# Block transposes through DRAM for the second batch of an attention and token-mixing kernel

## The chip, the cores and the metric

One Trainium2 chip, one core of it. The metric is the device time of one execution in microseconds (us); the median of several runs is given, and one more execution is profiled. TensorE (PE) multiplies matrices and also transposes by multiplying with an identity; VectorE (DVE), ScalarE (ACT) and GpSimd (POOL) work elementwise; SyncE (SP) issues almost all transfers, in one queue and in order. The five work side by side and wait for each other by semaphores.

## The reference

Four batches, 8 heads, 768 positions, head dimension 64. First attention in a window of 16 positions to both sides, with 24 more columns, one for each block of 32 positions (the maximum of its keys, the mean of its values). Then a mixer: an MLP over the tokens (768 to 256 to 768) with a residual, and an MLP over the channels (512 to 1536 to 512) with a residual.

```python
k_sum = k.reshape(B, H, nb, block, D).max(axis=3)
v_sum = v.reshape(B, H, nb, block, D).mean(axis=3)
scores_l = scale * np.matmul(q, k.transpose(0, 1, 3, 2))
mask_l = np.abs(pos[:, None] - pos[None, :]) < window
scores_s = scale * np.einsum('bhsd,bhnd->bhsn', q, k_sum) + np.log(block)
scores_all = np.concatenate([np.where(mask_l, scores_l, -1e9), scores_s], axis=-1)
a = np.exp(scores_all - np.max(scores_all, axis=-1, keepdims=True))
a = a / (np.sum(a, axis=-1, keepdims=True) + 1e-09)
x = np.matmul(a, np.concatenate([v, v_sum], axis=2))   # heads side by side: (B, S, 512)
...
xt = x.transpose(0, 2, 1)
h = np.maximum(xt @ w_tok1, 0.0) @ w_tok2
u = x + h.transpose(0, 2, 1)
h2 = np.maximum(u @ w_ch1, 0.0) @ w_ch2
return (u + h2).astype(np.float32)
```

## The kernel before, in words

The channel MLP is the bulk. It runs batch by batch, each batch in two halves of its tokens (512 and 256 columns; 384 and 384 in the last batch), and each half in 12 slots, one for each 128 of the 1536 hidden channels: `ch1` (12 matmuls into a bank hp), relu and a split into a high and a low part (ACT L851, DVE L856), `ch2` (12 matmuls added to banks acc). Numbers are carried as two float32r parts, so that each product takes three matmuls.

The attention of the next batch runs inside the MLP of the batch before it. A batch has four pairs of heads (p in the code, `NP` = 4 for each batch), and each pair two halves g of its tokens. The steps, 20 for a batch, are

- "s", `scores`: 24 matmuls (L428) into two banks sc, the minimum with the mask on DVE (L442) into a tile e, the exponential in place on ACT (L452). The tile e is 128 queries by 2 heads by 3 blocks of 128 columns, 120 of them used.
- "e", `turn` or `turn_blocks`: e must stand with its columns on the partitions for the next product; the result is eT.
- "a", `weighted`: 48 matmuls av (L559) of eT and v, scaled on DVE (L571) into x, and for some batches `turn_x` behind it. After it the next pair's v is loaded.

`ORDER` and `LATER` are two lists of these steps: `ORDER` puts the next pair's scores between the two "e" steps of a pair, `LATER` puts both "e" steps ahead of them. When all pairs are done, `tok1x` (PE L736, with splits xs and ws on ACT L717 and POOL L722) and `tok2` (PE L771, L779) make the token MLP and u. The first channel matmul of a batch needs u of all four pairs, of its half. The half with the higher tokens is made in slots 2 to 5 of the batch's own MLP. In the first batch's MLP the attention of the second is spread over a stretch from unit 20 to unit 30 (`a0`, `a1`, units of 256 columns; 36 in a batch), that is slots 10 to 17, since the weights are still being prepared ahead of it; in the later ones it is spread over units 0 to 29. `tok1x` stands in slots 20 and 22, `tok2` in slot 23 of the first batch's MLP.

Tiles come from rings: a tag such as "e" has 3 buffers, and the i-th tile of a tag can be written when tile i - 3 has been read for the last time. e, eT (from the second batch on), xb and the first half's xT all take buffers of "e". The order of instructions on each engine is written down beforehand: every piece of work is given to `Plan` with its engine, an assumed duration and a rank, a list scheduler runs through them with these durations (`RATE` and `LAND` for transfers), and each engine's queue is then fixed in the order of the assumed starts. Ranks go from `R_H` (scores, flips, weighted sums) down to `R_W` (the channel matmuls). `FAR` is the first batch that is turned by `turn_blocks` and `turn_x`.

```python
def att_step(b, s, behind=()):
    kind, hp, g = (LATER if b >= FAR else ORDER)[s]
    p = b * NP + hp
    if kind == "e":
        (turn_blocks if b >= FAR else turn)(p, g)
    elif kind == "a":
        weighted(p)
        if b >= FAR:
            turn_x(b, hp)
...
# in the loop over slots
if b >= FAR and u1s[p] == slot + 1: fetch_x(b, 1, p)
...
if b + 1 >= FAR: fetch_x(b + 1, 0, p)
tok2(b + 1, 0, p)
```

Of the kernel before, what the change touches and what calls it, by code (L numbers as in the profile page):

```python
# [188 lines left out]
def tile_attention_mixer(  # L189
# [22 lines left out]
    def sbuf(shape, tag, name, bufs, dtype=F32):  # L212
        return plan.slot(sb, shape, dtype, tag, name, bufs)
# [188 lines left out]
    def scores(p, g, behind=()):  # L402
# [3 lines left out]
        e = e_t[p, g] = sbuf([P, 2, HS], "e", f"e_{p}_{g}", 3)  # L406
        if p >= FAR * NP:

# [59 lines left out]
                )  # L468


    FAR = 2
    PARTS = [(j, i) for j in range(2) for i in range(TT // 2)]

    def turn(p, g):
# [126 lines left out]
# [10 lines that stand above are left out]
# [17 lines left out]
    def turn_x(b, p):  # L628

        x2, a = x_t[b, p]  # L630
        e = sbuf([P, S], "e", f"xb_{b}_{p}", 3)
        add(
            "dve", 1.05,
            lambda: nc.vector.transpose(
                e.t.rearrange("p (t c) -> p t c", c=P), x2.t[:, :, a, :]
            ),
            reads=x_keys(b, p), writes=[(e, 0)], rank=R_ATT,
        )
        for half, nt in enumerate(HT[b]):
            cs = slice(H0[b][half], H0[b][half] + nt)  # L640
            away = xa_t[b, half, p] = plan.slot(
                dram, [P, nt], F32, f"xaway{nt}", f"xaway_{b}_{half}_{p}", 8
            )
            add(
                "sp", 0.4, lambda away=away, cs=cs: nc.sync.dma_start(out=away.t, in_=e.t[:, cs]),
                reads=[(e, 0)], writes=[(away, 0)], kb=nt // 2,
            )

    def fetch_x(b, half, p):
        tag, bufs = (("e", 3), ("ot", 2))[half]  # L650
        slot = xT_t[b, half, p] = sbuf([P, HT[b][half]], tag, f"xT_{b}_{half}_{p}", bufs)
        fetch(xa_t.pop((b, half, p)), slot, lambda: slot.t, HT[b][half] // 5)
# [489 lines left out]
    for b in range(B):  # L1142
# [12 lines left out]
        for slot, (half, f) in enumerate(seq):  # L1155
            state["phase"] = half
            for p in range(NP):
                if b >= FAR and u1s[p] == slot + 1:
                    fetch_x(b, 1, p)
# [31 lines left out]
            if not last:  # L1191
# [7 lines left out]
                for p in range(NP):  # L1199
                    if slot == t2s[p]:  # L1200
                        if b + 1 >= FAR:
                            fetch_x(b + 1, 0, p)
# [66 lines left out]
```

## Time and profile before

| | |
|---|---|
| median of three runs | 581.9 us (580.58 to 582.2) |
| profiled execution, first to last instruction | 579.3 us; its own time is not listed apart from the runs |
| PE, DVE, ACT, POOL busy | 565.0, 288.2, 216.0, 154.1 us |
| mean granted TensorE clock | 0.994 of full speed |
| packets of under 512 B | 86640 of 116778 |
| bytes moved, mean rate | 75.89 MB, 131 GB/s |

Rows of groups read: line, engine, operation, written and read tile, shape and count; then busy time, mean of one in ns; then the engine's idle time just before them and what ended it. Rows of a timeline read: start and length in us, engine, line, operation, count. Rows of windows read: the stretch, its length, busy us and instructions of PE, of PE's weight loads, of DVE, ACT and POOL, the granted clock, the DMA engines' busy share and the rate in GB/s. SPq is SP's queue of transfers; a row there is the time that issuing took, not that of the transfer. L12 is line 12 of the kernel.

### The profile page before, as it was taken

To read this page: it belongs to the slowest core of one execution; us is meant where nothing else is said; L and a number is where in the kernel's file an instruction comes from. 1 tells how busy PE (TensorE), PEld (TensorE's weight loads), DVE (VectorE), ACT (ScalarE), POOL (GpSimd) and SP (SyncE) were. 2 spreads that over 40 slices of the span, in tenths; PEclk is the share of its full clock that TensorE was granted. 3 is DMA by queue.
4 is the path that set the end of the run, shared out by engine and by line. 5 is a ranking of instruction groups with operands and counts; after the bars stand their busy time and mean duration, and the time that the engine had idled before them with its cause. 6 is when DMAs were issued, how large, how long until landed. Compare 5 with 4: busy or idle time off the path is not lost.

```text
span 579.3 us, 12315 instructions
## 1 busy us (share of the span) xinstructions
PE 565.0 (98%) x4701; PEld 500.2 (86%) x4701; DVE 288.2 (50%) x872; ACT 216.0 (37%) x697; POOL 154.1 (27%) x191
## 2 busy tenths in 40 slices
PE   7889999989999999999999999999999999999997
PEld 4678888768999988878899988888799999999997
DVE  3698799997563255644743336452543222112112
ACT  4777565436474343322333224222434111111110
POOL 0236586743033310000085010100085022005000
PEclk9999999989999999999999999999999999999999
DMA  8954568653565027846775127746454012001001
GB/s 281 325 159 129 182 200 262 220 164 129 188 190 161 18 76 197 230 121 188 204 192 131 23 55 189 195 139 139 117 146 81 1 34 59 1 1 54 1 1 54
DMA packets 116778, 75.89 MB, mean 131 GB/s; under 512 B 86640, under 2 KB 100080, under 8 KB 116720
## 3 DMA queue, kind: packets, MB, share of 16 engines
q1 hardware_dynamic: 116432, 74.72, 45.6%
q8 instruction: 37, 0.61, 0.4%
q10 hardware_dynamic: 288, 0.39, 0.2%
q14 instruction: 21, 0.17, 0.1%
HBM read 57.59 MB, written 15.73 MB: 127 GB/s over the span
## 4 chain that ended last, share of the span: by engine, by line
PE 82%; DVE 11%; DMA 3%; issue 2%; ACT 1%; SPq 0%; POOL 0%; DVEq 0%; ACTq 0%
PE acc L882 31%; PE hp L839 30%; PE t1q L736 5%; PE up L779 4%; PE av L559 4%; PE sc L428 4%; DMA w<-in_w_ch 2%; DVE wb L1067 2%; DVE wp L1060 1%; PE et L490 1%; PE warm L1108 1%; DVE wp L1053 1%; DVE wb L1060 1%; DVE vs L384 1%; DVE e L442 1%
## 5 line engine op out<-in xcount | busy, mean ns | idle before, releaser
L882 PE MATMUL acc<-h,w2h 128*128 128x512 f32 (+2 forms) x768 | 207.1, 340 | 2.2 <-DVE h L856 2.2
L839 PE MATMUL hp<-u,w1h 128*128 128x512 f32 (+2 forms) x768 | 192.7, 338 | 0.0
L882 PEld LDWEIGHTS acc<-h,w2h 128*128 128x128 f32 x768 | 135.8, 189 | 17.0 <-DVE h L856 3.4
L839 PEld LDWEIGHTS hp<-u,w1h 128*128 128x128 f32 x768 | 132.6, 189 | 12.3 <-issue 1.3
L856 DVE SCALAR_TENSOR_TENSOR h<-hp,h 128x512 fp32r<-128x512 f32 (+2 forms) x96 | 53.1, 553 | 153.8 <-ACT h L851 153.8
L839 PE MATMUL hp<-u,w1l 128*128 128x512 f32 (+2 forms) x384 | 129.1, 336 | 0.3 <-POOL w1l L1095 0.3
L882 PE MATMUL acc<-h,w2l 128*128 128x512 f32 (+2 forms) x384 | 129.1, 336 | 0.0
L851 ACT ACTIVATE h<-hp 128x512 fp32r<-128x512 f32 (+2 forms) x96 | 46.9, 488 | 201.4 <-PE hp L839 200.4
L452 ACT ACTIVATE e<-e,den 128x120 f32<-128x120 f32 x192 | 73.3, 385 | 48.6 <-DVE den L442 41.1
L839 PEld LDWEIGHTS hp<-u,w1l 128*128 128x128 f32 x384 | 72.5, 189 | 6.6 <-POOL w1l L1095 0.7
L882 PEld LDWEIGHTS acc<-h,w2l 128*128 128x128 f32 x384 | 72.6, 189 | 5.2
L943 POOL TENSOR_TENSOR ot<-ot,u 128x512 f32<-128x512 f32 (+2 forms) x28 | 27.9, 1021 | 116.8 <-DVE ot L935 116.8
L442 DVE CUSTOM_DVE_ANT_0 e<-sc,mask_sb 128x120 f32<-128x120 f32 x192 | 41.4, 277 | 13.7 <-PE sc L428 10.9
L779 PE MATMUL up<-wt2h,t 128*128 128x256 f32 (+2 forms) x128 | 37.6, 351 | 0.5 <-DVE xT L795 0.5
L411 POOL MEMSET e<- 128x48 f32 x16 | 2.2, 138 | 130.1 <-DMA away<-e 69.5
L452 ACT ACTIVATION_READ_ACCUMULATOR e<-e,den 128x1 f32 x192 | 36.3, 189 | 0.0
L722 POOL TENSOR_TENSOR xs<-x,xs 128x512 fp32r<-128x512 f32 x18 | 23.5, 1304 | 27.8 <-ACT xs L717 27.7
L428 PE MATMUL sc<-k,q 64*64 64x120 f32 x768 | 28.6, 275 | 1.9 <-PE et L490 0.7
L428 PEld LDWEIGHTS sc<-k,q 64*64 64x64 f32 x768 | 21.0, 134 | 10.5 <-issue 6.8
L736 PE MATMUL t1q<-xs,ws 128*128 128x256 f32 x216 | 28.9, 284 | 0.0
L559 PEld LDWEIGHTS av<-v,eT 120*64 120x64 f32 x768 | 24.0, 138 | 4.8 <-issue 2.3
L736 PEld LDWEIGHTS t1q<-xs,ws 128*128 128x128 f32 x216 | 27.3, 191 | 0.3
(73 smaller groups left out, 597.0 us busy)
## 6 DMA issues: line engine op xcount, KB each, us to landing
w<-in_w_ch SPq DMA_DIRECT2D x48, 256.0 KB
k<-in_kw SPq DMA_DIRECT2D x16, 720.0 KB
v<-in_vw SPq DMA_DIRECT2D x32, 288.0 KB
q<-in_q SPq DMA_DIRECT2D x16, 384.0 KB
away<-e SPq DMA_DIRECT2D x16, 384.0 KB
eT<-away SPq DMA_DIRECT2D x64, 96.0 KB
w<-in_w_tok SPq DMA_DIRECT2D x12, 256.0 KB
vb<-in_vb SPq DMA_DIRECT2D x32, 96.0 KB
```

The costliest lines, as they stand in the source:

```text
L428: nc.tensor.matmul(tiles[j].t[c * QT : (c + 1) * QT, i * NC : (i + 1) * NC], lhsT=qt.t[rows, t * QT : (t + 1) * QT], rhs=kt.t[rows, t, :], ...
L442: nc.vector.tensor_tensor_reduce(out=e.t[:, j, i * P : i * P + NC], in0=tiles[j].t[:, i * NC : (i + 1) * NC], in1=mask_sb[:, mv, :], op0=A ...
L452: nc.scalar.activation(ei, ei, AF.Exp, bias=den_t[n].t[:, 1, T : T + 1], scale=-1.0, accum_out=den_t[n].t[:, 0, T : T + 1],)
L559: nc.tensor.matmul(pv[cs, T], lhsT=eT[:NC, T % (TT // 2), cs], rhs=v.t[:NC, 2 * T + c], start=True, stop=True,)
L722: lambda slot=slot, src=src: nc.gpsimd.tensor_tensor(out=slot.t[:, 1], in0=src(), in1=slot.t[:, 0].bitcast(F32), op=ALU.subtract),
L736: nc.tensor.matmul(pt.t[:, 2 * P * k : 2 * P * (k + 1)], lhsT=ws[:, wp, T, ks], rhs=xs[:, xp, T], start=(c == 0 and k == 0 and T == 0 and ...
L779: nc.tensor.matmul(pt.t[:, :nt], lhsT=t1.t[:, part, ks], rhs=w[:, k, h0 : h0 + nt], start=(far and k == 0 and i == 0), stop=(k == DTOK // ...
L839: nc.tensor.matmul(pt.t[:, :nt], lhsT=w[:, c, fs], rhs=us[c].t[:, part], start=(i == 0), stop=(i == len(ops) - 1),)
L851: lambda: nc.scalar.activation(h.t[:, 0], pt.t[:, :nt], AF.Relu),
L856: lambda: nc.vector.scalar_tensor_tensor(out=h.t[:, 1], in0=pt.t[:, :nt], scalar=0.0, in1=h.t[:, 0].bitcast(F32), op0=ALU.max, op1=ALU.sub ...
L882: nc.tensor.matmul(slot.t[:, c0 : c0 + nt], lhsT=w[:, f, o * P : (o + 1) * P], rhs=h.t[:, part], start=(f == 0 and w is w2h and part == 0 ...
L943: lambda view=view, u=u: nc.gpsimd.tensor_tensor(out=view(), in0=view(), in1=u.t[:, 1].bitcast(F32), op=ALU.add),
```

## The change

`FAR` goes from 2 to 1, so the second batch (b = 1) takes the path of the third and fourth.

```diff
-    FAR = 2
+    FAR = 1
```

What this exchanges for b = 1:

- `turn` flips each e on PE (three matmuls with the identity for each head, L490) into a bank and copies it to eT on ACT (L501). `turn_blocks` transposes the 32 by 32 blocks of e in place on DVE (L513), writes the tile to DRAM (away, L517, 384 KB) and fetches it in four transfers (L532, 96 KB each, in runs of 32 numbers), one for each group of 32 partitions, so that the blocks land where the full transpose has them. `scores` also zeroes the unused columns of e on POOL (L411).

```python
def turn_blocks(p, g):
    e = e_t[p, g]
    away = plan.slot(dram, [P, 2 * HS], F32, "away", f"away_{p}_{g}", 3)
    t_sb = sbuf([P, 2, HS], "e", f"eT_{p}_{g}", 3)
    ...
    add("dve", 1.05, lambda: nc.vector.transpose(flat(e.t), flat(e.t)), ...)
    add("sp", 0.4, lambda: nc.sync.dma_start(out=away.t, in_=flat(e.t)), ...)
    fetch(away, t_sb, lambda: flat(t_sb.t), 150)

def fetch(away, slot, view, kb):
    def part(r):
        rows = slice(32 * r, 32 * (r + 1))
        src = away.t.rearrange("(q p) (t k) -> p t q k", p=32, k=P)
        nc.sync.dma_start(
            out=view()[rows].rearrange("p (t q c) -> p t q c", q=P // 32, c=32),
            in_=src[..., rows])
    for r in range(P // 32):
        add("sp", 0.4, lambda r=r: part(r), reads=[(away, 0)], writes=[(slot, r)], kb=kb)
```

- The residual's x was transposed inside `tok2` on PE (L771) into the bank of the token MLP. Now `turn_x` transposes the blocks of x on DVE (L634) into a tile xb and writes both halves to DRAM (xaway, L645), and `fetch_x` brings each back as xT in four transfers. `tok2` adds bank and xT on DVE (L795), copies the high part of u on ACT (L802) and subtracts on DVE or, in the second half, on POOL (L808).
- The steps of b = 1 come in the order `LATER` instead of `ORDER`.

## The prediction

> **What bounds the kernel now.** I read the page first: busy shares, then the chain that ended last.
>
> ```profile
> span 579.3 us, 12315 instructions
> PE 565.0 (98%) x4701; PEld 500.2 (86%) x4701; DVE 288.2 (50%) x872; ACT 216.0 (37%) x697; POOL 154.1 (27%) x191
> PE 82%; DVE 11%; DMA 3%; issue 2%; ACT 1%; SPq 0%; POOL 0%; DVEq 0%; ACTq 0%
> ```
>
> PE is the bound as an average, so an instruction taken off PE is worth its own time, but only where the PE queue has other work ready. The second batch's attention runs inside the first batch's MLP, so the stretch that decides is from its first scores to the first matmul of its MLP. I took that stretch from the timeline of PE, the chain in order of time, and the table by windows.
>
> ```profile
> 128.38 0.85 PE L428 MATMUL sc<-k,q 64*64 64x120 f32 x24
> 145.24 1.55 PE av L559 x48
> 178.88 1.55 PE av L559 x48
> 206.50 0.63 PE L839 MATMUL hp<-u,w1h 128*128 128x512 f32 x2
> 145.00:185.00 40.00, 40.00 (x557) 37.93 (x556) 22.35 (x102) 23.36 (x87) 8.05 (x9) 1.00 0.63 193
> 185.00:205.00 20.00, 20.00 (x148) 18.80 (x147) 6.36 (x14) 6.94 (x15) 8.32 (x8) 1.00 0.07 18
> ```
>
> In the window rows the first pair is length and busy PE. The second batch's scores begin at 128.38, its four pairs of heads finish their weighted sums (L559) from 145.24 to 178.88 + 1.55 = 180.4, one pair every (178.88 - 145.24) / 3 = 11.2 us, and its MLP (512 columns wide) begins at 206.50. PE never idles between 145 and 205. So there are 206.5 - 180.4 = 26.1 us between the last weighted sum and the MLP, all of it filled, and the attention has that much room at most. The third batch starts at 209.35 and has some 125 us of MLP to hide in; the second has only what is left of the first batch's MLP.
>
> **The change, part by part.** Removed from PE: the flips of e (L490), three matmuls for each of 16 tiles, 48 in all, and the residual's transposes (L771), 16 in the first half and 8 in the second.
>
> ```profile
> 135.75 0.82 PE L490 MATMUL et<-identf,e 128*120 128x128 f32 x6
> 136.32 0.36 PE L839 MATMUL hp<-u,w1h 128*128 128x256 f32 x1
> 190.51 0.60 PE L771 MATMUL up<-identf,x 128*128 128x128 f32 x4
> 190.86 0.51 PE L779 MATMUL up<-wt2h,t 128*128 128x512 f32 x1
> ```
>
> Six flips hold the queue 136.32 - 135.75 = 0.57 us, 0.095 each: 48 x 0.095 = 4.6 us. Four residual transposes hold it 0.35 us, 0.088 each: 16 give 1.4, the 8 of the second half 0.7. PE sheds 6.7 us; with the cover intact that is the gain. ACT also loses its 16 copies of eT.
>
> Added elsewhere, from the groups by form and from the tiles' views (shortest/median/longest, ns):
>
> ```profile
> L513 DVE STREAM_TRANSPOSE e<-e 128x768 f32<-128x768 f32 x16 | 15.6, 976 | 11.5 <-ACT e L452 11.2
> L634 DVE STREAM_TRANSPOSE xb<-x 128x768 f32<-128x768 f32 x8 | 7.8, 979 | 0.3
> L411 POOL MEMSET e<- 128x48 f32 x16 | 2.2, 138 | 130.1 <-DMA away<-e 69.5 <-PE av L559 41.5 <-PE et L490 10.3
> L532 SPq DMA_DIRECT2D eT<-away x64: 557/652/3628, 221.0 to 426.3; - x64
> L517 SPq DMA_DIRECT2D away<-e x16: 327/374/593, 214.9 to 420.2; - x16
> L645 SPq DMA_DIRECT2D xaway<-xb x16: 421/497/653, 237.1 to 435.4; - x16
> L532 SPq DMA_DIRECT2D xT<-xaway x64: 557/622/1198, 308.8 to 484.1; - x64
> ```
>
> Per batch: DVE gets 8 x 0.98 + 4 x 0.98 = 11.7 us of block transposes, and in tok2 one more addition for each u. In the second half the subtraction goes to POOL. POOL gets 8 memsets, 1.1 us. All three engines are half idle in these windows (DVE 22.35 of 40 us), so I cost that work at nothing where it stands beside PE, and count it only where it lies in the chain below. SP's queue gets 8 x 0.37 + 32 x 0.65 + 8 x 0.50 + 32 x 0.62 = 47.7 us of issuing, some 27 us of it before the last weighted sum. It is one queue in order: k, q, v, vb and the third batch's preparations wait behind each fetch that waits for its trip to DRAM.
>
> The price is in the latency of one pair of heads. The ring "e" has three buffers, and e, eT and xb now all turn in it. The second e of a pair can be written only when the previous pair's second eT has been read by its weighted sum, so the chain of a pair is closed: weighted sum, scaling, turning x, minimum, exponential, block transpose, write to DRAM, four fetches, weighted sum. Nothing of it runs ahead. The third batch shows it under the same loads of k, q, v and vb:
>
> ```profile
> 209.35 0.85 PE L428 MATMUL sc<-k,q 64*64 64x120 f32 x24
> 230.68 1.55 PE av L559 x48
> 255.42 1.55 PE av L559 x48
> 263.56 0.98 DVE L513 STREAM_TRANSPOSE e<-e 128x768 f32<-128x768 f32 x1
> 264.31 0.69 SPq L270 DMA_DIRECT2D k<-in_kw  x1
> 265.05 0.43 SPq L270 DMA_DIRECT2D q<-in_q  x1
> 265.58 0.38 SPq L517 DMA_DIRECT2D away<-e  x1
> 273.16 1.97 SPq L532 DMA_DIRECT2D eT<-away  x3
> 275.87 0.56 SPq L532 DMA_DIRECT2D eT<-away  x1
> 278.25 1.59 PE av L559 x48
> 305.05 1.55 PE av L559 x48
> ```
>
> From the first scores to the end of the first weighted sum: 230.68 + 1.55 - 209.35 = 22.9 us. From one weighted sum to the next: 278.25 - 255.42 = 22.8 and 305.05 - 278.25 = 26.8. In the first of these the write went out behind k and q, its first fetch came 273.16 - 265.58 = 7.6 us later, the last fetch was issued at 276.43, and the weighted sum at 278.25 is a piece of the chain that ended last: this interval is not just slack in the schedule. Where k and q were farther ahead, the trip was shorter:
>
> ```profile
> 243.74 0.33 SPq L517 DMA_DIRECT2D away<-e  x1
> 247.38 2.67 SPq L532 DMA_DIRECT2D eT<-away  x4
> ```
>
> that is 6.3 us from the write's issue to the last fetch's end. Lower end for a pair: the present 11.2, plus 0.98 and 6.3, less the flips and copies that go (0.57 and some 0.9): 17, and I put 16 so that an overlap is allowed for. Upper end: the mean of 22.8 and 26.8, 24.8. I take 20, nearer to 22.8, since the loads are the same and the ring is the same, and a little below it because PE's order added about 1 us there and the third batch was not pressed for time.
>
> Last weighted sum of the second batch: 128.4 + 22.9 + 3 x 20 = 211.3, instead of 180.4. The first batch's MLP does not wait for it and runs out at 206.5 - 4.6 - 1.4 = 200.5. Behind the last weighted sum lies what the MLP needs: the splits of x for tok1x, tok1x, tok2, and the residual's fetch. The third batch again gives the length:
>
> ```profile
> 327.40 0.69 DVE L808 TENSOR_TENSOR u<-xT,u 128x512 fp32r<-128x512 f32 x1 [0.75 <-ACT u L802]
> 319.02 2.37 SPq L532 DMA_DIRECT2D xT<-xaway  x3
> ```
>
> The last u there is done at 328.1, 328.1 - 306.6 = 21.5 us behind the weighted sum, with MLP matmuls between. Its last fetch of xT ended at 321.4, held back because the fourth xT takes the ring's buffer from the first; addition, copy and subtraction follow (about 2 us, and 2 for landing): 18.9 us at least by that path. Without the MLP in between I take 18.5 and keep 17 and 21.5 as ends. So the second batch's MLP starts at 211.3 + 18.5 = 229.8 instead of 206.5: 23.3 us late, with PE idle for most of 29 us.
>
> After an idle PE the clock is lower for a while:
>
> ```profile
> 117.00:119.00 2.00, 0.18 (x2) 0.16 (x2) 2.00 (x6) 1.12 (x3) 1.19 (x2) 1.00 0.57 198
> 119.00:121.00 2.00, 2.00 (x6) 1.51 (x7) 1.97 (x5) 0.14 (x2) 0.99 (x2) 0.52 0.97 329
> 121.00:123.00 2.00, 2.00 (x7) 1.62 (x6) 2.00 (x4) 0.73 (x2) 1.53 (x2) 0.62 0.58 183
> ```
>
> Granted clock (third column from the right) 0.52 and 0.62 in 4 us cost 2 x 0.48 + 2 x 0.38 = 1.7 us; bounds 0 and twice that, taken once. Sum: +23.3 + 1.7 - 0.7 = +24.3. The third and fourth batches have room (their attention is spread over a whole MLP), so the delay is carried to the end unchanged. The profiled span of 579.3 becomes 603.6. The median of the runs, 581.9, lies 2.6 above the span; I carry that over: 606.
>
> How much of the pair's 20 us is the short runs of the fetches (32 numbers of 4 bytes at a time) shows in the table by windows, whose last two columns are DMA share and GB/s:
>
> ```profile
> 218.00:220.00 2.00, 2.00 (x11) 1.63 (x10) 1.90 (x4) 0.23 (x1) 0.00 (x0) 1.00 0.99 390
> 226.00:228.00 2.00, 2.00 (x14) 1.75 (x13) 0.41 (x2) 0.63 (x2) 0.00 (x0) 1.00 0.79 126
> ```
>
> With k and q under way the queues moved 390 GB/s at a share of 0.99; with fetches of eT alone 126 at 0.79, 160 for full share. 384 KB take 2.5 us at the one rate and 1.0 at the other. At the higher rate the two fetches of a pair would be 3 us shorter, a pair 17 and the time 597. The Trainium skill, "DMA: Bandwidth & Descriptors", section Specifications, gives 512 B as the least transfer for line rate; by that rule the 128 B runs stay at the low rate, the trace agrees (126 against 390), and the sum is the 606 and not the 597. The Trainium skill, "VectorE: DVE Perf Modes", section Rules for kernel authors, also speaks against the change: it sends a 128x128 transpose to TensorE where PSUM will do as its target, which here is the 0.57 us on PE against the trip of 6.3 to 7.6 us.
>
> **The rivals.** *Hidden (faster).* The round trip fits beside the MLP that is left. Then the second batch's MLP starts at 200.5, PE keeps all 6.7 us and the time is 575. It decides by the pair's interval: 200.5 - 18.5 = 182, so (182 - 151.3) / 3 = 10.2 us for a pair; break-even is near 12.5. For it speaks that the planner sets a new order; against it that 11.2 is today's interval without the trip, and that the ring closes the chain. Chance 0.10, of which 0.02 lands within 0.3%.
>
> *Short trip.* The chain of a pair runs at its lower end, 16, and the tail at 17: 128.4 + 22.9 + 48 + 17 = 216.3, 9.8 late, less 0.7: the time is 591. For it speaks the 6.3 us trip; against it the same loads packed into less time. Chance 0.20.
>
> *Queue in order (slower still).* SP waits for one write with the next pair's loads behind it, as where one fetch took 3628 ns to issue. 24.8 for a pair and 21.5 behind: 128.4 + 22.9 + 74.4 + 21.5 = 247.2, 40.7 late, less 0.7 and plus 1.7: 624. Chance 0.12.
>
> **How the numbers follow.** The forecast, 606, has 0.58, with a range of its own of 596 to 616 (a pair at 17 to 23). The range 590 to 620 takes in the short trip and leaves out the hidden case and the upper end of the queue case, 0.18 together. About 0.3%, 1.7 us, is what a measurement of this kernel can tell from no change. Faster 0.08, same 0.02, slower 0.90.
>
> **What would show it.** The profile after: no flips beyond the first batch's 48, 24 block transposes of e and 12 of x, 96 fetches of eT. Weighted sums of the second batch some 20 us apart, the last ending near 211. PE idle, waiting for e, DMA or t1q's splits, some 29 us between 150 and 232, and a dip of the granted clock behind it. The MLP of the second batch starts near 230, everything after keeps its spacing. The prediction is wrong if the weighted sums stand 12 us apart or less, if the first batch's MLP does not run out before they end, or if the second batch's scores start well before 128.

## The result and the profile after

The changed kernel takes 608.8 us (median of 4 runs, 606.8 to 609.25) against 582.05 before: ratio 1.0445, interval 1.0412 to 1.0479. It is slower by 26.8 us. The profiled execution spans 606.5 us, 27.2 more than before.

First the page of the changed kernel: span, busy shares, and from the 40 slices PE's busy tenths and its granted clock.

```profile
span 606.5 us, 12360 instructions
PE 563.1 (93%) x4629; PEld 497.8 (82%) x4629; DVE 302.4 (50%) x888; ACT 209.9 (35%) x681; POOL 158.4 (26%) x203
...
PE   7789999899972579999999999999999999999997
...
PEclk9999999999995778999999999999999999999999
```

PE has 72 instructions fewer and its share falls from 98% to 93%. The two lines of slices (15.2 us each) say where: a hole in slices 13 to 15 (182 to 227 us), with the granted clock down to half in it. Elsewhere the PE line stays within a tenth or two of that of the kernel before. The groups and a tile's view show that the instructions moved as the code says:

```profile
L490 PE MATMUL et<-identf,e 128*120 128x128 f32 x48 | 8.3, 288 | 3.5 <-ACT e L452 3.4
L513 DVE STREAM_TRANSPOSE e<-e 128x768 f32<-128x768 f32 x24 | 23.4, 976 | 14.8 <-ACT e L452 14.4
L532 SPq DMA_DIRECT2D eT<-away x96: 557/654/2144, 138.0 to 454.7; - x96
```

The weighted sums of the second batch and the first matmul of its MLP, from PE's timeline:

```profile
149.32 1.76 PE L559 MATMUL av<-v,eT 120*64 120x64 f32 x48
172.63 1.62 PE L559 MATMUL av<-v,eT 120*64 120x64 f32 x48
195.26 2.19 PE L559 MATMUL av<-v,eT 120*64 120x64 f32 x36 [4.10 <-DMA eT<-away]
...
233.04 0.62 PE L839 MATMUL hp<-u,w1h 128*128 128x512 f32 x2
```

and the end of the attention, from the chain in order of time:

```profile
196.29 5.96 DMA v<-in_vw
...
202.26 1.42 SPq L532
203.73 1.25 SPq L532
...
205.08 3.38 DMA away<-e
208.47 0.56 SPq L532
...
211.17 2.58 DMA eT<-away
213.89 2.20 PE av L559 x36
```

The weighted sums end at 151.1, 174.2, 197.5 and 216.1: 21.7 us apart on the mean (before: 11.2). No PE row stands between the last two in this stretch of the chain: SP's fetches, the write of e to DRAM, the fetch back. The chain puts the last two of the four fetches ahead of that write (1.42 and 1.25 us of issuing against a median of 0.65) behind v's transfer. Before this stretch the chain holds SP's issuing alone, from 180.31 to 193.03. SP's queue there:

```profile
179.10 2.42 SPq L532 DMA_DIRECT2D xT<-xaway  x3
181.57 2.72 SPq L532 DMA_DIRECT2D eT<-away  x4
...
188.34 1.88 SPq L532 DMA_DIRECT2D xT<-xaway  x3
190.26 2.72 SPq L532 DMA_DIRECT2D eT<-away  x4
```

Fetches of x for the second half, which are needed only once the second batch's MLP runs, stand directly ahead of the fetches of eT.

The MLP starts at 233.04 instead of 206.50, 26.5 us later, and that is nearly the whole 27.2. Counted from the second batch's first scores it takes 108.2 us in place of 78.1, which is 30.0 more: in this run the scores began 3.5 us earlier, at 124.88. The windows:

```profile
160.00:180.00 20.00, 18.24 (x219) 17.25 (x217) 12.41 (x44) 8.76 (x33) 4.68 (x6) 1.00 0.87 222
180.00:200.00 20.00, 4.70 (x72) 4.05 (x72) 7.89 (x35) 3.05 (x15) 3.68 (x7) 0.54 0.80 204
200.00:215.00 15.00, 8.66 (x69) 8.24 (x71) 4.88 (x17) 3.52 (x14) 2.82 (x3) 0.73 0.78 171
215.00:233.00 18.00, 15.03 (x81) 12.14 (x79) 6.79 (x11) 5.77 (x11) 7.71 (x7) 0.79 0.59 122
sum 108.00, PE 81.49 PEld 73.09 DVE 56.34 ACT 34.27 POOL 25.96; mean PE 13.58 PEld 12.18 DVE 9.39 ACT 5.71 POOL 4.33
```

The sum is over 125 to 233 (the rows before 160 are left out): PE is idle for 108.0 - 81.5 = 26.5 us there. Of the engines that took the work over, DVE is busy for half of the stretch (56.3 us) and POOL for a quarter. The transfer engines are at 0.78 to 0.87 from 160 to 215, and at 0.59 behind that.

What the ring of three buffers does shows on POOL, whose memset is the first to write a new e (from its timeline):

```profile
174.32 0.14 POOL L411 MEMSET e<- 128x48 f32 x1 [7.42 <-PE av L559]
197.52 0.14 POOL L411 MEMSET e<- 128x48 f32 x1 [9.89 <-PE av L559]
```

So the second e of a pair does wait for the weighted sum of the pair before. It is not the only thing that holds it there: DVE has the scaling of that sum (197.49) and the turning of x (198.09) ahead of the minimum that fills this e (198.99), in its own fixed order.

### The profile page after: what moved, and what is told of

It is laid out like the page before. It is cut to its first block, busy times and chain, and to the rows that moved or that the text cites. A ratio compares the mean times of both kernels' runs of the same rounds, so it can differ in the third digit from the quotient of the medians.

```text
span 606.5 us, 12360 instructions
## 1 busy us (share of the span) xinstructions
PE 563.1 (93%) x4629; PEld 497.8 (82%) x4629; DVE 302.4 (50%) x888; ACT 209.9 (35%) x681; POOL 158.4 (26%) x203
## 4 chain that ended last, share of the span: by engine, by line
PE 67%; DVE 9%; DMA 9%; SPq 6%; ACT 4%; issue 3%; POOL 2%; DVEq 0%; ACTq 0%; POOLq 0%
PE acc L882 26%; PE hp L839 26%; SPq L532 5%; PE av L559 4%; PE up L779 4%; PE t1q L736 3%; PE sc L428 3%; DMA w<-in_w_ch 2%; DMA v<-in_vw 2%; ACT e L452 2%; DVE wb L1067 1%; DVE wp L1060 1%; DVE wp L1053 1%; DMA k<-in_kw 1%; DVE wb L1060 1%
## 5 line engine op out<-in xcount | busy, mean ns | idle before, releaser
L856 DVE SCALAR_TENSOR_TENSOR h<-hp,h 128x512 fp32r<-128x512 f32 (+2 forms) x96 | 53.0, 552 | 151.3 <-ACT h L851 151.2
L779 PE MATMUL up<-wt2h,t 128*128 128x256 f32 (+2 forms) x128 | 39.3, 366 | 3.1 <-ACT t L670 1.6
L559 PE MATMUL av<-v,eT 120*64 120x64 f32 x768 | 29.4, 235 | 11.6 <-DMA eT<-away 10.2
L411 POOL MEMSET e<- 128x48 f32 x24 | 3.3, 138 | 141.0 <-PE av L559 61.8
L559 PEld LDWEIGHTS av<-v,eT 120*64 120x64 f32 x768 | 26.4, 147 | 16.0 <-issue 9.4
L428 PEld LDWEIGHTS sc<-k,q 64*64 64x64 f32 x768 | 21.1, 135 | 21.0 <-issue 17.4
L736 PE MATMUL t1q<-xs,ws 128*128 128x256 f32 x216 | 31.3, 300 | 4.8 <-ACT e L452 2.8
L736 PEld LDWEIGHTS t1q<-xs,ws 128*128 128x128 f32 x216 | 29.4, 206 | 5.8 <-ACT e L452 2.9
```

Of the source, the lines that this page charges most:

```text
L428: nc.tensor.matmul(tiles[j].t[c * QT : (c + 1) * QT, i * NC : (i + 1) * NC], lhsT=qt.t[rows, t * QT : (t + 1) * QT], rhs=kt.t[rows, t, :], ...
L559: nc.tensor.matmul(pv[cs, T], lhsT=eT[:NC, T % (TT // 2), cs], rhs=v.t[:NC, 2 * T + c], start=True, stop=True,)
L736: nc.tensor.matmul(pt.t[:, 2 * P * k : 2 * P * (k + 1)], lhsT=ws[:, wp, T, ks], rhs=xs[:, xp, T], start=(c == 0 and k == 0 and T == 0 and ...
L779: nc.tensor.matmul(pt.t[:, :nt], lhsT=t1.t[:, part, ks], rhs=w[:, k, h0 : h0 + nt], start=(far and k == 0 and i == 0), stop=(k == DTOK // ...
L856: lambda: nc.vector.scalar_tensor_tensor(out=h.t[:, 1], in0=pt.t[:, :nt], scalar=0.0, in1=h.t[:, 0].bitcast(F32), op0=ALU.max, op1=ALU.sub ...
```

## The experiments

Theory A: the chain of one pair of heads through DRAM, closed by the ring of three buffers, sets the pace. Rival B: the order of the steps (`LATER`) does. Rival C: the traffic does, either by the engines' time (C1) or by SP's issuing in order (C2). Intervals below are between the ends of the second batch's weighted sums, as a mean of three.

In all edits `FAR` is split in three: `FAR_E` for e's turning, `FAR_X` for x's, `FAR_O` for the order.

**The order alone.**

```diff
+    FAR_E, FAR_X, FAR_O = 2, 2, 1
```

> Only the order of the second batch's steps is changed to LATER; e is flipped and x transposed on PE as before. Theory A (the closed chain of a pair through DRAM costs the time) expects about the time of the kernel before, 580 to 584 us, weighted sums of the second batch 10 to 13 us apart. Rival B (the order of the steps does it) expects 600 us or more with weighted sums 18 us or more apart. Rival C (SP's queue and the transfers' volume do it) expects 580 to 584 us, as there are no new transfers.

583.0 us, ratio 1.0026 (1.0005 to 1.0048). From PE's timeline, the first and last of the four sums and the MLP's start:

```profile
144.19 1.62 PE L559 MATMUL av<-v,eT 120*64 120x64 f32 x48
...
177.21 1.62 PE L559 MATMUL av<-v,eT 120*64 120x64 f32 x48
207.69 0.63 PE L839 MATMUL hp<-u,w1h 128*128 128x512 f32 x2
```

(177.21 - 144.19) / 3 = 11.0 us apart. The order alone costs a quarter of a per cent, half a per cent at the most. B is out.

**e alone through DRAM.**

```diff
+    FAR_E, FAR_X, FAR_O = 1, 2, 1
```

> e of the second batch goes through DRAM, order LATER; the residual's x stays on PE. Theory A expects most of the loss: weighted sums 19 to 22 us apart, 602 to 608 us. Rival C expects clearly less of the loss, since the write-outs of x (4 x 384 KB) and 32 fetches of x in SP's queue are gone: weighted sums 16 to 18 us apart, 592 to 600 us.

605.0 us, ratio 1.038 (1.0329 to 1.0431). The chain's last rows:

```profile
214.24 2.19 PE av L559 x36
231.63 2.75 PE hp L839 x12
```

The first sum ended at 154.0, so the intervals are 20.8. From the first scores (127.28) to the MLP it takes 104.2 us, 4.0 less than in the changed kernel. Turning e makes most of the loss, 23.6 us on the kernel before as it was measured beside this run. Taking 32 fetches and 8 writes of x out of SP's queue shortened a pair by 0.9 us, where C expected intervals of 16 to 18.

**x alone through DRAM.**

```diff
+    FAR_E, FAR_X, FAR_O = 2, 1, 1
```

> Only the residual's x of the second batch goes through DRAM, order LATER; e is flipped on PE. Theory A expects no stall to speak of, because x's trip is needed only at the end: weighted sums 10 to 14 us apart, 2.1 us of PE work gone, 578 to 583 us. Rival C expects part of the loss, 586 to 592 us, as SP issues 40 more transfers.

590.1 us, ratio 1.015 (1.0117 to 1.0183): A's number failed and C's held. The chain in order of time says by what:

```profile
162.20 8.38 DMA xaway<-xb
...
170.69 0.50 ACT eT L501
...
171.23 1.62 PE av L559 x48
```

ACT's copy of eT waited for the write of x: eT takes the buffer of "e" that xb still held, and this write took 8.4 us to land. Intervals are 14.5 us, just above A's 10 to 14. So a trip that nothing reads for a long time entered the chain through a shared ring.

**eT from another ring.**

```diff
-        t_sb = sbuf([P, 2, HS], "e", f"eT_{p}_{g}", 3)
+        tag, n = ("u0", 4) if p < 2 * NP else ("e", 3)
+        t_sb = sbuf([P, 2, HS], tag, f"eT_{p}_{g}", n)
```

> The whole change, but eT of the second batch takes its four buffers from another ring (u0), so that the second e of a pair need not wait for the weighted sum of the pair before. The first eT must wait for the first batch's first half to be finished (about 145), and part of the splits for tok1x move behind the last weighted sum (some 5 us). Theory A expects weighted sums 13 to 17 us apart, 594 to 604 us. Rival C expects that transfers set the pace: still 19 to 22 us apart, 608 to 615 us.

614.0 us, ratio 1.0559 (1.0522 to 1.0596), slower still. PE's timeline:

```profile
152.98 1.62 PE L560 MATMUL av<-v,eT 120*64 120x64 f32 x48
180.42 1.62 PE L560 MATMUL av<-v,eT 120*64 120x64 f32 x48
...
220.56 2.19 PE L560 MATMUL av<-v,eT 120*64 120x64 f32 x36 [4.62 <-DMA eT<-away]
```

Intervals of 22.7 us, not the 13 to 17 that A expected of an opened ring; the time is in C's range. But the chain was not opened. From the timelines of POOL and DVE, before the last sum:

```profile
197.42 0.14 POOL L411 MEMSET e<- 128x48 f32 x1 [14.12 <-DMA away<-e]
205.13 0.56 DVE L572 TENSOR_TENSOR x<-av,rec 128x384 f32<-128x384 f32 x1 [0.72 <-PE av L560]
206.62 0.24 DVE L442 CUSTOM_DVE_ANT_0 e<-sc,mask_sb 128x120 f32<-128x120 f32 x1
```

The memset waits for a write to DRAM now and no longer for the weighted sum, so the new ring did what it was for. The minimum, whose scores were done at 187.7 and whose buffer was free at 197.6, still came at 206.62, because DVE's fixed order has the scaling of the previous sum ahead of it. The planner also made another order elsewhere (the second sum was reached at 180.42 without a wait, behind MLP matmuls). So the run says nothing on what an open chain would cost, and what the ring alone costs is not shown.

**No loads of k and q.** Pairs 6 to 9 use the tiles of an earlier pair, so this run computes other scores; it is for its time only.

```diff
     def load_k(p):
         b, hp = divmod(p, NP)
+        if 6 <= p < 10:
+            k_t[p] = k_t[p - 2]
+            return None
```

(`load_q` likewise.)

> The whole change, but the k and q of pairs 6 to 9 aren't loaded: these pairs use the tiles of the pair two before (the loads of 1.1 MB per pair are left out, so their numbers are those of another pair). The issuing of SP shrinks by only 0.8 us per pair. If the transfer engines' time sets the pace of a pair (C1), the weighted sums come 16 to 19 us apart and the time is 592 to 600 us. If SP's queue of issues sets it (C2), they stay 20 to 22 us apart and the time is 603 to 608 us. If the pure latency of the chain does (A), 604 to 609 us.

602.1 us, ratio 1.0345 (1.0293 to 1.0397), intervals of 19.2. Its chain holds one interval in which no MLP matmul stands, from a weighted sum to the next:

```profile
189.07 2.20 PE av L565 x36
191.88 0.98 DVE xb L640
193.22 2.01 ACT e L458 x10
195.70 0.98 DVE e L519
196.97 0.91 SPq L270
198.58 2.77 DMA away<-e
203.39 2.90 DMA eT<-away
206.42 2.20 PE av L565 x36
```

206.42 - 189.07 = 17.4 us: the closed chain that A names, without k and q in front of the write (2.77 us to land; 3.38 in the changed kernel). The time and the intervals lie between the ranges that were expected, and the gain on the changed kernel is 6.8 us: the loads of k and q have a part, not the whole.

**The second half's fetches held.** The profile after shows eight fetches of x for the second half in the midst of the attention, put there by the planner because their data was ready. Here they wait for the second batch's MLP.

```diff
-                    fetch_x(b, 1, p)
+                    fetch_x(b, 1, p, [at])   # planned behind ch1 of its slot
```

> The whole change, but the fetches of x for the second batch's second half are held until that batch's MLP has begun; the profile after shows 8 of them (0.6 us of SP each, 256 KB in all) between 176 and 190, in the midst of the attention. C2 (SP's queue) expects some 5 us less, 602 to 605 us. C1 (the engines' time) expects 1 to 3 us less, 606 to 608 us. A expects no change, 608 to 610 us.

604.1 us, ratio 1.0374 (1.0326 to 1.0422): 4.7 us less than the changed kernel, within C2's range and outside C1's and A's. Intervals of 20.2, 60.7 for three in place of 65.0. So eight fetches in the wrong place of SP's queue cost about what their issuing takes, 8 x 0.6 = 4.8 us.

**v and vb from POOL's queue.**

```diff
-        load(slot, lambda t: t[:WIN], vw[b, h], 295)
+        load(slot, lambda t: t[:WIN], vw[b, h], 295, pool=10 <= n < 18)   # nc.gpsimd.dma_start; vb of b == 2 too
```

> The whole change, but the loads of v for pairs 5 to 8 and of vb for the third batch are issued by POOL's queue in place of SP's: the same bytes through the same engines, some 2.5 us of issuing less on SP per pair, and no fetch behind a v load that waits. C2 expects 2 to 4 us less per pair, 597 to 603 us. C1 expects 606 to 611 us. A expects 607 to 610 us.

613.2 us, ratio 1.0521 (1.0477 to 1.0565). No gain from 2.5 us less issuing per pair; intervals of 22.6. C2's expectation failed. The eight fetches of x still stood ahead of eT's in this run, and POOL's own queue got a new order; what each share was is not separated.

**Both holds.** No k and q, and the second half's fetches held; again the scores of other pairs.

> Both: no loads of k and q for pairs 6 to 9 (they use another pair's), and the fetches for the second half held until the second batch's MLP has begun. What is left of an interval is the chain itself with the loads of v and vb. A (a floor of 16 to 17.5 us for the chain of a pair through DRAM, whatever the traffic) expects three intervals of 16 to 18.5, a last weighted sum ending near 203 and 595 to 599 us. If traffic were all (C1), the intervals would fall to the 11 us of the kernel before and the time to 585 us or less.

597.2 us, ratio 1.0267 (1.021 to 1.0324), within A's range. PE's timeline:

```profile
152.97 1.62 PE L565 MATMUL av<-v,eT 120*64 120x64 f32 x48
...
206.50 2.19 PE L565 MATMUL av<-v,eT 120*64 120x64 f32 x36 [3.60 <-DMA eT<-away]
224.80 0.62 PE L845 MATMUL hp<-u,w1h 128*128 128x512 f32 x2
```

Intervals of 18.0 (152.97 + 1.62 to 206.50 + 2.19), within A's 16 to 18.5; the last sum ended at 208.7 and not near 203, since the first scores began only at 129.9. Traffic was not all: 11 did not come back. Nor was it little: 11.6 of the 26.8 us went with these loads and fetches. The last interval, 16.7, is the shortest of all runs with e through DRAM, and its chain has no load in it but 0.25 us of issuing one: scaling, turning x, minimum, exponential, block transpose, write (2.84 us to land), fetches, weighted sum. That is the length of the chain of a pair with a quiet queue.

**Half of eT's fetches from ACT's queue.**

```diff
-            nc.sync.dma_start(
+            (nc.scalar if act(r) else nc.sync).dma_start(   # r = 1, 3; held fetches as above
```

> Second-half fetches held as before, and two of the four fetches of each eT of the second batch issued by ACT's queue, so that a fetch takes 1.3 us of issuing in place of 2.7; the same bytes and the same round trip. If SP's issuing is part of the chain (C2), an interval shortens by 1.3 to 2.6 us against the run with the fetches held (604.1), 597 to 601 us. If the engines' time or the latency of the trip sets it, 603 to 606 us. ACT waits in order for the trip to DRAM; if that delays exponentials, the time is above 606 us.

602.7 us, ratio 1.0371 (1.0325 to 1.0418), 1.4 less than with the hold alone and between the two expectations. The last sum begins at 210.35 against 212.28. Halving the issuing of eT's own fetches is worth little; with two intervals that overlap it is not shown to be worth anything.

**x alone, from another ring.** e is flipped on PE in the old order; only x goes through DRAM, its turned tile in a ring that is free at that time.

```diff
+    FAR_E, FAR_X, FAR_O = 2, 1, 2
-        e = sbuf([P, S], "e", f"xb_{b}_{p}", 3)
+        tag, n = ("h", 2) if b == 1 else ("e", 3)
+        e = sbuf([P, S], tag, f"xb_{b}_{p}", n)
```

> e of the second batch is flipped on PE as before and in the order of before; only its residual's x goes through DRAM, and the turned x takes its buffers from the ring h, which the first batch's second half leaves free, so that no eT waits for the write of x. If the loss of the run with x alone (590 us) came through the shared ring, weighted sums are 10 to 12 us apart and the time is 578 to 582 us, by 2.1 us of PE work less than before. If it came from SP's queue (x's fetches behind vb and v), 585 to 590 us.

583.5 us, ratio 1.0033 (1.0004 to 1.0062), between the two ranges. The sums stand 11.0 us apart (143.71 to 176.58), so the wait of the run with x alone is gone. This run has the old order as well as the other ring, but the order alone had 11.0 too, and the chain above named the shared buffer. But the time is no better than before. With the second half's fetches held as above as well:

> e of the second batch flipped on PE, in the order of before; its residual's x through DRAM from the ring h, and the fetches of the second half held until its MLP has begun, so that SP issues only what the first half needs behind the last weighted sum. If SP's queue ate the 2.1 us of PE work that x's trip saves (583.5 us without the hold, against 582.4 for the kernel before), 578.5 to 581 us. If not, 582 to 584 us.

579.0 us, ratio 0.9949 (0.9924 to 0.9973): half a per cent faster than the kernel before, and the fastest of all. From 125 to 200 its PE never idles:

```profile
180.00:200.00 20.00, 20.00 (x149) 19.04 (x149) 9.87 (x20) 8.02 (x17) 10.30 (x9) 1.00 0.52 115
200.00:208.00 8.00, 7.71 (x57) 7.16 (x56) 5.09 (x11) 1.54 (x3) 1.53 (x4) 1.00 0.18 43
...
206.88 0.63 PE L840 MATMUL hp<-u,w1h 128*128 128x512 f32 x2
```

The MLP starts at 206.88 and in the kernel before at 206.50, but the first scores began at 130.03 and there at 128.38. Counted from them it starts 1.3 us sooner (76.85 against 78.12), which is about the 1.4 us of the first half's 16 transposes. The 2.9 us of the medians are somewhat more than the 2.1 us that left PE; the interval of 1.6 to 4.4 us holds both, and where the rest comes from is not shown.

## Why the prediction was right

606 was forecast, 608.8 measured; slower, within the range, and by the path that was named: e's trip through DRAM stretches a pair, and PE runs out of work. That the number came within 3 us is in part luck. From the first scores to the MLP 101.4 us were forecast and 108.2 measured, and half of this miss was made good by scores that began early. Step by step:

- *PE's work fell by 72 instructions* as counted, and none of it was seen as a gain: the cover was gone.
- *The first weighted sum* ends at 151.1, forecast 151.3. Two errors cancelled: the scores began at 124.9 and not 128.4, and took 26.2 us and not 22.9. The early start goes with that run's clock and not with the change: the first scores began at 124.9 to 126.2 in the three profiled runs with a granted clock of 1.00 all through the first 60 us (the changed kernel is one), and at 129.9 to 130.4 in the three that had 0.83 in the first 20 us. So the sign "scores well before 128" came true, and it tells nothing here.
- *An interval* was put at 20 us; it measured 21.7, 65.0 for three in place of 60. This is the term that was too small, by 5 us. The count of SP's issuing put some 27 us ahead of the last sum and no fetch of the second half's x among them; eight stood there. With them held, three intervals take 60.7; with no x through DRAM at all, under another plan, 62.4. So x's transfers account for 2.6 to 4.3 of the 5 us. The bounds of 16 and 24.8 hold the mean of every run in which e goes through DRAM.
- *What lies behind the last sum* was put at 18.5; it took 233.04 - 216.08 = 17.0, the lower end. The path was the one named, fetches of xT, their landing, addition, copy, subtraction. The hold of the fourth xT that the 18.5 allowed for is not on this chain.
- *The clock* cost was put behind the hole. It lies in it: granted 0.54 between 180 and 200 and 0.79 between 215 and 233, and full from 233 on. The last 10 of tok2's 12 matmuls take 4.14 us there (229.06 to 233.20); 12 took 2.80 in the third batch of the kernel before, which is 2.33 for 10; so about 1.8 us of this kind are inside the 17.0. The size of the term, 1.7, was thus near for this one place, and its place in the sum was wrong.
- *The MLP that is left* was said to run out at 200.5. It ran out at 178.2, and PE was mostly idle from there on (4.70 us busy of 20): what filled it until 206.5 before included tok1x and tok2 of the second batch, which wait for the same sums. They ran inside the hole, so that the idle time came to 26.5 us, near the 29 that were forecast with the wrong start. The sum did not use the 200.5.
- *The reason for the interval.* Shown: e's trip makes it (20.8 with e alone, 11.0 with the order alone), and 18.0 remain without k, q and the second half's fetches. Of the 10.7 us that an interval grew (11.0 with the order alone, 21.7), 7 stay with the chain and v's and vb's traffic, and 3.7 go with the loads and fetches taken away; how much of the 3.7 is the engines' time and how much SP's issuing is not separated. The ring's wait is there (9.89 us on POOL), but DVE's order closes the chain as well, and with eT in another ring the intervals were 22.7. Not shown: what the ring alone costs, and what v and vb do, since no run leaves them out.
- *The short runs of the fetches* as the reason for their rate, 126 against 390 GB/s, were not tested. SP's issuing bounds that rate too: 96 KB in 0.65 us are 151 GB/s.

The rival with the short trip (16 for a pair, 591) was near the floor for a quieter queue: 17.4 and 16.7 in the last intervals of the two runs without k and q. The hidden case needed 10.2, and no run with e through DRAM came below 16.7 for a single interval. The rival of the queue in order had a part of what happened, though at 4.7 us and not at the 18 by which its 624 lies above the forecast.

## What to carry to other kernels

Before an engine's work is moved to a longer path, measure the interval that the stage has and the one that the path needs: here 11 against 17 at the least and 22 with the loads in the queue, and some 6.7 us of saved PE work became 27 us of loss. The same change is worth its saving where what travels is needed only at the end: x alone, with its buffers in a ring that was free and the later fetches kept out of the queue, made the kernel 0.5% faster (0.3 to 0.8). In a queue that is issued in order, a transfer that is ready early but needed late delays the ones behind it: eight of them cost 4.7 us. A write that nobody waits for still delays whoever takes its buffer next.

## What the runs showed of the hardware

The write of one turned tile of x (two transfers, 384 KB) took 8.4 us until it let its buffer go, when k and q had been issued just ahead of it (160.73 and 161.26 on SP in that run). Issuing itself can stretch: a fetch of eT that takes SP 0.65 us at the median took 1.42 and 1.25 us at 202.26 and 203.73, behind two loads of v and two writes of x issued from 196.29 on, and 2144 ns at the longest. What stretches it is not separated. The granted clock in the first 20 us was 1.00 in some profiled runs and down to 0.83 in others of the same first stage, and the first scores began between 124.9 and 130.4 us with it.
